# Block fetches behind the transposition, and u loaded in halves a step later

## The chip, the cores and the metric

One core of a Trainium2 chip. The time is the device time of one execution in microseconds (us). TensorE (PE) multiplies 128x128 weights with up to 512 columns into PSUM, VectorE (DVE) and ScalarE (ACT) do the elementwise work, SyncE (SP) and GpSimd (POOL) issue the DMAs. Each engine runs its own instructions in the order of the program and waits on semaphores for the others. SP's DMAs all go into one queue, worked off by 16 DMA engines.

## The reference

```python
def _attn_ref(u, v, z):                      # u, v: 4 x 3008 x 256, z: 4 x 3008 x 64
    scores = (1.0 / S) * np.matmul(z, z.transpose(0, 2, 1))
    attn = np.maximum(scores, 0.0) ** 2
    out = np.matmul(attn, v)
    return (u * out).astype(np.float32)

def _moe_ref(x, w_in, w_out):                # 12032 x 256, 256 x 2048, 2048 x 256
    h = x @ w_in
    relu6 = np.clip(h + 3.0, 0.0, 6.0)
    g = h * relu6 / 6.0
    return (g @ w_out).astype(np.float32)
```

The result is `_moe_ref(_attn_ref(u, v, z).reshape(12032, 256), w_in, w_out)`. All is done to float32 accuracy: each operand of a matmul is split into a rounded high and a low part.

## The kernel before, in words

**Work and order.** The order of all instructions is written out by hand in one loop over 288 steps (called g, from 0): 4 batches (b) of 6 chunks of 512 query tokens (c; the sixth has 448) of 12 pairs of 128-token key blocks (p). Step g multiplies the attention of pair g with v into two PSUM banks, `o0` and `o1` (d = 0 and 1, the halves of the 256 features), and computes the scores of pair g + 2. At the last step of a chunk, `times_u` (L560) multiplies `o0` and `o1` in place into the tile of u; only then may the first matmul of the next chunk write that bank.

**Mirrored blocks.** The score matrix is symmetric. A computed block that will be wanted transposed is stored to DRAM (`keep`, tiles `d`), later fetched with four DMAs (`fetch_pair`, L342, tile `l`, two buffers) and transposed on DVE (`turn`, L381, tile `rm`). Step g transposes the block of pair g + 3, ahead of which at most two fetched blocks wait; `fetch_mirrored` at the end of a step issues the next fetch where a buffer is free. In the sixth chunk ten of the twelve pairs are mirrored, ten steps in a row.

**MLP.** From step 33 on, every three steps hold one group: 128 x 2 of the 2048 hidden features of 1024 tokens (two chunks). A group's first step (on = 0) begins with two loads on SP, `wi` of the next group and `wo` of this one (L238, 896 and 512 KB). Its products `m` are spread over the three steps; its four `y` products (`down`) follow from the end of its third step. After 8 groups the output is scaled on ACT (L669) and stored (L672).

**u.** The tile of u has one buffer, for 1024 tokens: 1 MB, or 960 KB for a sixth chunk. After the last product with u, `split_x` turns the tile into the operands of the MLP in the first three steps behind a pair of chunks (`since` 1 to 3; the last subtraction, `xl` at L88, at the end of the third); then `load_u` (L552) fetches the next u. That load stands at the end of the third of these steps, three steps ahead of the step with the first products with the new u, which is the last one of the pair's first chunk. (The first two loads stand in steps 7 and 32.) The step after the load is always a group's first step (on = 0); in it SP also issues two stores of the computed blocks of the chunk's last pair (256 and 128 KB) and the output store of 512 KB.

**The code of a step** with on = 0: scores of pair g + 2 (first half), products with v for d = 0, `background()` (which transposes), the group's first part with the loads of `wi` and `wo`, the other half of the scores with the stores, products with v for d = 1, further parts of the group, `down()`, `fetch_mirrored()`, `load_u`. With on = 2 (the last step of a chunk): a part of the group, products for d = 0 and the first product with u, a part of the group, `down()`, scores, `background()`, scores, a part of the group, products for d = 1 and the second product with u, `down()`.

Of the kernel before, what the change touches and what calls it, by code (L numbers as in the profile page):

```python
# [7 lines left out]
F32 = mybir.dt.float32  # L8
# [7 lines left out]
P = 128  # L16
CH = 512
NCH = 6
# [9 lines left out]
SPLIT_FROM = 24  # L28
# [11 lines left out]
def relu2_attention_then_hswish_mlp(  # L40
# [24 lines left out]
    upool = ctx.enter_context(tc.tile_pool(name="upool", bufs=1))  # L65
# [234 lines left out]
    def flush():  # L300
        while late:
            late.pop(0)()
# [20 lines left out]
    to_fetch = []  # L323

    def fetch_mirrored():

        while to_fetch and len(mirrored) < 2:
            b, c, p = to_fetch[0]
            if (b, p // 2, c) not in whole:
                return  # L330
            fetch_pair(*to_fetch.pop(0))

    def fetch_pair(b, c, p):


        src = kept[b, p // 2, c]
        half = is_half(b, c, p)
        nk = 8 if half else width(c) // 32
        t = lpool.tile([P, 16, 64], F32, tag="l", name="l")
        for q in range(4):  # L340
            c0 = q * 64 if half else q * P + (p % 2) * 64
            nc.sync.dma_start(  # L342
                out=t[32 * q:32 * q + 32, :nk, :],
                in_=src[:, c0:c0 + 64].rearrange("(k e) f -> e k f", e=32),
            )
        mirrored[b, c, p] = t
# [195 lines left out]
    raw_x = {}  # L542

    def tokens(i):

        b, c = divmod(i, NCH // 2)
        return b * S + 2 * c * CH, width(2 * c) + width(2 * c + 1)

    def load_u(i):
        t0, n = tokens(i)  # L550
        t = raw_x[i] = upool.tile([P, 2, 2 * CH], F32, tag="u", name="u")
        nc.sync.dma_start(  # L552
            out=t[:, :, :n], in_=ut[:, t0:t0 + n].rearrange("(k p) t -> p k t", p=P)
        )

    def times_u(b, c, d):
# [7 lines left out]
    def split_x(i):  # L564


        raw = raw_x[i]
        n = tokens(i)[1] // 2
        left, right = raw[:, :, :n], raw[:, :, n:2 * n]
        new = xt[i] = {}  # L570

        def piece(k, src):
            shape = [P, 2, CH] if k < 3 else [P, CH]
            homes = ((xpool, f"xh{k}"), (xpool, f"xl{k}"))
            if i == NPR - 1:
                homes = ((apool, "ah"), (apool, "al")) if k < 3 else ((zpool, "zx"), (zpool, "zy"))
            xh, xl = (
                pool.tile(shape, F32R, tag=tag, name=f"x{w}{k}")
                for (pool, tag), w in zip(homes, "hl")
            )  # L580
            hi, lo = (x[:, :, :n] if k < 3 else x[:, :n] for x in (xh, xl))
            nc.scalar.copy(out=hi, in_=src)
            for r in range(2 if k < 3 else 1):
                new[2 * k + r] = (hi[:, r], lo[:, r]) if k < 3 else (hi, lo)
            return lambda: sub(lo, src, f(hi))

        if i < NPR - 1:
            pool, tag = (rpool, "r") if i else (hpool, "hb")
            t = pool.tile([P, 2, CH], F32, tag=tag, name="t")[:, :, :n]
        else:  # L590
            t = lpool.tile([P, 16, 64], F32, tag="l", name="t")
            t = t.rearrange("p k f -> p (k f)").rearrange("p (r n) -> p r n", r=2)[:, :, :n]
        sub(t[:, 0], right[:, 1], right[:, 0])
        sub(right[:, 0], right[:, 0], left[:, 0])
        sub(t[:, 1], right[:, 1], right[:, 0])
        yield
        low = piece(0, left)
        yield
        low()
        sub(left[:, 1], left[:, 1], t[:, 1])  # L600
        yield
        low = piece(2, t)
        yield
        low()
        yield
        low = piece(1, right)
        yield
        low()
        yield
        low = piece(3, left[:, 1])  # L610
        yield
        low()
        raw_x.pop(i)
        yield
# [207 lines left out]
    def turn_next():  # L822

        while g_turned[0] < min(g_done + 1, len(pairs)):
            turn(*pairs[g_turned[0]])
            g_turned[0] += 1

    def run(it, n=99):
        for _ in range(n):
            next(it, None)  # L830
# [9 lines left out]
    with tc.manual_schedule():  # L840
# [12 lines left out]
        second = scores(0, 0, 1, banks=("y10", "y11"))  # L853
# [5 lines left out]
        for i, (b, c) in enumerate(chunks):  # L859
            ahead = b + 1 if c == NCH - 1 and b + 1 < B else None  # L860
            for p in range(NPAIR):
                g = i * NPAIR + p
# [28 lines left out]

                def background():
                    turn_next()
                    if i == 0 and p == 7:
                        load_u(0)

                def prepare():
                    if ahead and p < NPAIR - 1:
# [18 lines left out]
                if on < 2 or at_mlp < 0:  # L917
# [5 lines left out]
                    else:  # L923
# [3 lines left out]
                        split_z(0, 2)  # L927
                    spare()
                    background()
                    run(unit, 1)  # L930
                    spare()
# [15 lines left out]
                else:  # L947
# [5 lines left out]
                    down()  # L953
                    run(nxt, 1)
                    background()
                    run(nxt, 1)
                    spare()
# [13 lines left out]
                done, since = divmod(g + 1 - AFTER, NFP * EVERY)  # L971
                if g == SPLIT_FROM:
                    xs = split_x(0)
                if SPLIT_FROM <= g < SPLIT_FROM + 9:
                    run(xs, 1)
                if g == SPLIT_FROM + 8:
                    load_u(1)
                if done > 1 and since in range(1, 4):
                    if since == 1:
                        xs = split_x(done - 1)  # L980
                    run(xs, 3)
                    if since == 3:
                        load_u(done)
        flush()
        xs = split_x(NPR - 1)
        left = range((len(pairs) - MLP_FROM) // EVERY, NPR * NFP)
# [96 lines left out]
```

## Time and profile before

| | |
|---|---|
| median of 3 runs | 1833.07 us (1832.08 to 1834.41) |
| the profiled execution | 1833.69 us, span 1831.9 us |
| granted TensorE clock, mean | 0.998 |
| PE busy | 1801.4 us (98%) |
| PEld (weight loads) | 1584.7 us (87%) |
| DVE | 1505.2 us (82%) |
| ACT | 1196.3 us (65%) |
| POOL | 55.2 us (3%) |
| DMA | mean 180 GB/s; SP's queue 60.8% of 16 engines' span |

Busy shares are of the span. A matmul's row shows some 0.38 us, since its ends are modelled and matmuls overlap; one of 512 columns starts every 0.215 us. In the rows, L73 is the helper of all matmuls and L88 that of all subtractions, so tiles tell them apart.

### The profile page before, as it was taken

To read this page: it belongs to the slowest core of one execution; us is meant where nothing else is said; L and a number is where in the kernel's file an instruction comes from. 1 tells how busy PE (TensorE), PEld (TensorE's weight loads), DVE (VectorE), ACT (ScalarE), POOL (GpSimd) and SP (SyncE) were. 2 spreads that over 40 slices of the span, in tenths; PEclk is the share of its full clock that TensorE was granted. 3 is DMA by queue.
4 is the path that set the end of the run, shared out by engine and by line. 5 is a ranking of instruction groups with operands and counts; after the bars stand their busy time and mean duration, and the time that the engine had idled before them with its cause. 6 is when DMAs were issued, how large, how long until landed. Compare 5 with 4: busy or idle time off the path is not lost.

```text
span 1831.9 us, 23310 instructions
## 1 busy us (share of the span) xinstructions
PE 1801.4 (98%) x8426; PEld 1584.7 (87%) x8426; DVE 1505.2 (82%) x1767; ACT 1196.3 (65%) x1640; POOL 55.2 (3%) x90
## 2 busy tenths in 40 slices
PE   8999999999999999999999999999999999999999
PEld 7877888988998888888899888888889988888888
DVE  8999988988778788897877877888877787787776
ACT  7896655767656555676766655667675665564565
POOL 1000000100000000010000000001000000000000
PEclk9999999999999999999999999999999999999999
DMA  8868896665664767856665667594565667676343
GB/s 227 242 220 264 212 221 183 188 190 172 183 159 140 193 168 152 229 161 202 186 178 135 177 176 178 130 258 151 160 202 144 173 186 175 143 171 162 109 167 128
DMA packets 440307, 329.50 MB, mean 180 GB/s; under 512 B 278656, under 2 KB 397440, under 8 KB 440192
## 3 DMA queue, kind: packets, MB, share of 16 engines
q1 hardware_dynamic: 432672, 304.16, 60.8%
q0 software_dynamic: 7520, 23.86, 4.5%
q8 instruction: 66, 1.08, 0.3%
q14 instruction: 49, 0.40, 0.1%
HBM read 241.70 MB, written 86.25 MB: 179 GB/s over the span
## 4 chain that ended last, share of the span: by engine, by line
PE 56%; issue 24%; DVE 11%; ACT 4%; DMA 2%; SPq 1%; POOL 0%; DVEq 0%; ACTq 0%; POOLq 0%
PE o L73 22%; PE y L73 16%; PE m L73 14%; PE s L73 5%; DVE al L88 2%; DMA l<-d 1%; DVE rm L381 1%; DVE gl L88 1%; DVE rb L706 1%; ACT gh L766 1%; DVE ra L706 1%; SPq L342 1%; DVE r L462 1%; DVE hb L91 1%; DVE xl L88 0%
## 5 line engine op out<-in xcount | busy, mean ns | idle before, releaser
L73 PE MATMUL m<-xh,wi 128*128 128x512 f32 (+1 forms) x1344 | 476.9, 378 | 8.0 <-DVE hb L91 4.4
L73 PE MATMUL o<-ah,vl 128*128 128x512 f32 (+1 forms) x1152 | 433.2, 376 | 9.8 <-DVE u L560 6.3
L73 PE MATMUL o<-ah,vh 128*128 128x512 f32 (+1 forms) x1152 | 432.0, 375 | 0.0
L73 PE MATMUL y<-gh,wo 128*128 128x512 f32 (+1 forms) x1536 | 388.6, 375 | 0.5 <-ACT gh L766 0.5
L73 PE MATMUL o<-al,vh 128*128 128x512 f32 (+1 forms) x1104 | 328.8, 376 | 2.9 <-DVE al L88 2.9
L73 PEld LDWEIGHTS y<-gh,wo 128*128 128x128 f32 x1536 | 289.9, 189 | 35.8 <-ACT gh L766 1.8
L73 PEld LDWEIGHTS m<-xh,wi 128*128 128x128 f32 x1344 | 254.9, 190 | 48.3 <-DVE hb L91 9.2
L73 PEld LDWEIGHTS o<-ah,vl 128*128 128x128 f32 x1152 | 217.7, 189 | 41.6 <-DVE u L560 8.7
L73 PE MATMUL m<-xl,wi 128*128 128x512 f32 (+1 forms) x672 | 252.4, 376 | 0.0
L73 PEld LDWEIGHTS o<-ah,vh 128*128 128x128 f32 x1152 | 218.0, 189 | 26.6
L73 PEld LDWEIGHTS o<-al,vh 128*128 128x128 f32 x1104 | 208.6, 190 | 30.0 <-DVE al L88 5.4
L73 PE MATMUL y<-gl,wo 128*128 128x512 f32 (+1 forms) x768 | 226.4, 376 | 0.9 <-DVE gl L88 0.5
L441 ACT ACTIVATE rt<-s 128x512 f32<-128x512 f32 (+1 forms) x310 | 180.0, 593 | 71.2 <-PE s L73 64.3
L462 DVE TENSOR_TENSOR r<-rt 128x1024 f32<-128x1024 f32 (+2 forms) x128 | 147.4, 1151 | 81.0 <-ACT rt L441 80.9
L747 ACT ACTIVATE ra<-m,three 128x512 f32<-128x512 f32 (+1 forms) x96 | 65.1, 678 | 174.9 <-PE m L73 132.0
L91 DVE TENSOR_TENSOR hb<-hb,m 128x512 f32<-128x512 f32 (+1 forms) x192 | 128.6, 670 | 59.7 <-PE m L73 59.0
L88 DVE TENSOR_TENSOR al<-r,ah 128x1024 fp32r<-128x1024 f32 (+3 forms) x147 | 164.3, 1118 | 5.7 <-ACT r L460 3.8
L469 ACT ACTIVATE ah<-rt 128x1024 fp32r<-128x1024 f32 (+1 forms) x155 | 163.7, 1056 | 4.9
L73 PEld LDWEIGHTS y<-gl,wo 128*128 128x128 f32 x768 | 144.7, 189 | 20.5 <-DVE gl L88 3.6
L88 DVE TENSOR_TENSOR gl<-rb,gh 128x1024 fp32r<-128x1024 f32 (+2 forms) x97 | 115.2, 1189 | 57.2 <-ACT gh L95 56.7
L381 DVE STREAM_TRANSPOSE rm<-l 128x1024 f32<-128x1024 f32 (+2 forms) x132 | 149.4, 1132 | 8.4 <-DMA l<-d 8.4
L88 DVE TENSOR_TENSOR al<-rm,ah 128x1024 fp32r<-128x1024 f32 (+1 forms) x132 | 155.2, 1176 | 1.3 <-ACT ah L408 0.9
(86 smaller groups left out, 2170.4 us busy)
## 6 DMA issues: line engine op xcount, KB each, us to landing
wi<-dwin SPq DMA_DIRECT2D x96, 896.0 KB, 5.4
d<-r SPq DMA_DIRECT2D x212, 256.0 KB, 3.2
wo<-dwout SPq DMA_DIRECT2D x96, 512.0 KB, 6.1
l<-d SPq DMA_DIRECT2D x304, 128.0 KB, 4.0
l<-d SPq DMA_DIRECT2D x160, 112.0 KB, 4.7
vraw<-in_v_dram POOLq DMA_DIRECT2D x33, 256.0 KB, 4.6
u<-in_ut_dram SPq DMA_DIRECT2D x8, 1024.0 KB, 5.4
out_dram<-y SPq DMA_DIRECT2D x16, 512.0 KB, 5.3
```

What stands on the lines that cost most here:

```text
L73: nc.tensor.matmul(out, lhsT=lhsT, rhs=rhs, start=start, stop=stop, skip_group_check=part)
L88: nc.vector.tensor_tensor(out=out, in0=a, in1=b, op=ALU.subtract)
L91: nc.vector.tensor_tensor(out=out, in0=a, in1=b, op=ALU.add)
L342: nc.sync.dma_start(out=t[32 * q:32 * q + 32, :nk, :], in_=src[:, c0:c0 + 64].rearrange("(k e) f -> e k f", e=32),)
L381: nc.vector.transpose(out=rn[:, :, :n].rearrange("p r (k e) -> p r k e", e=32), in_=t[:, :n // 32].rearrange("p k (r e) -> p r k e", r=2),)
L441: nc.scalar.activation(out=halved(rn[:, r]), in_=unpaired(s[:, :n]), func=AF.Relu, scale=1.0 / S)
L462: nc.vector.tensor_tensor(out=to, in0=of, in1=of, op=ALU.mult)
L469: nc.scalar.activation(out=hn, in_=rn, func=AF.Square)
L706: nc.vector.scalar_tensor_tensor(out=out, in0=out, scalar=6.0, in1=h, op0=ALU.min, op1=ALU.mult)
L747: nc.scalar.activation(out=ra[:, 1], in_=c21, func=AF.Relu, bias=three)
L766: nc.scalar.copy(out=ga[0], in_=ra)
```

## The change

`background()`, right behind the transposition, also calls `fetch_mirrored()` when the next block to fetch is one of a sixth chunk. `load_u` loads 512 columns at a time. For the third and later pairs of chunks the first half is issued at the end of the step behind the one where the whole load was, the second half seven steps after that. The first pair's second half comes twelve steps after its first, the second pair's eight steps.

```diff
-    def load_u(i):
+    def load_u(i, second):
+
         t0, n = tokens(i)
-        t = raw_x[i] = upool.tile([P, 2, 2 * CH], F32, tag="u", name="u")
+        if not second:
+            raw_x[i] = upool.tile([P, 2, 2 * CH], F32, tag="u", name="u")
+        cols = slice(CH, n) if second else slice(0, CH)
         nc.sync.dma_start(
-            out=t[:, :, :n], in_=ut[:, t0:t0 + n].rearrange("(k p) t -> p k t", p=P)
+            out=raw_x[i][:, :, cols],
+            in_=ut[:, t0 + cols.start:t0 + cols.stop].rearrange("(k p) t -> p k t", p=P),
         )
...
                 def background():
                     turn_next()
-                    if i == 0 and p == 7:
-                        load_u(0)
+                    if to_fetch and to_fetch[0][1] == NCH - 1:
+                        fetch_mirrored()
+                    if i < 2 and p == 7:
+                        load_u(0, i == 1)
...
-                if g == SPLIT_FROM + 8:
-                    load_u(1)
+                if g in (SPLIT_FROM + 8, SPLIT_FROM + 16):
+                    load_u(1, g == SPLIT_FROM + 16)
                 if done > 1 and since in range(1, 4):
                     if since == 1:
                         xs = split_x(done - 1)
                     run(xs, 3)
-                    if since == 3:
-                        load_u(done)
+                if done > 1 and since in (4, 11):
+                    load_u(done, since == 11)
```

## Rows read from the trace of the kernel before

**Rows 1.** Waits of PE: engine, tile and line, waited for: us in total, times, longest.
```profile
PE o L73 <- DVE u L560: 6.3, 4, 2.2
```
**Rows 2.** Timeline of PE around the four stops: start us, us, [idle before <-releaser].
```profile
300.48 1.03 PE L73 MATMUL y<-gh,wo 128*128 128x512 f32 x4
301.34 0.59 PE L73 MATMUL y<-gl,wo 128*128 128x512 f32 x2
...
305.96 0.52 PE L73 MATMUL o<-ah,vl 128*128 128x448 f32 x1 [2.24 <-DVE u L560]
...
754.78 0.46 PE L73 MATMUL o<-ah,vl 128*128 128x448 f32 x1 [0.86 <-DVE u L560]
...
1202.34 0.46 PE L73 MATMUL o<-ah,vl 128*128 128x448 f32 x1 [1.19 <-DVE u L560]
...
1650.63 0.46 PE L73 MATMUL o<-ah,vl 128*128 128x448 f32 x1 [2.04 <-DVE u L560]
```
**Rows 3.** Timeline of DVE ahead of the four stops, the first batch's in detail.
```profile
288.62 1.10 DVE L381 STREAM_TRANSPOSE rm<-l 128x896 f32<-128x896 f32 x1
...
298.50 0.68 DVE L560 TENSOR_TENSOR u<-u,o 128x512 f32<-128x512 f32 x1
...
303.09 1.11 DVE L381 STREAM_TRANSPOSE rm<-l 128x896 f32<-128x896 f32 x1 [2.77 <-DMA l<-d]
...
305.23 0.68 DVE L560 TENSOR_TENSOR u<-u,o 128x512 f32<-128x512 f32 x1
...
751.91 1.11 DVE L381 STREAM_TRANSPOSE rm<-l 128x896 f32<-128x896 f32 x1 [1.39 <-DMA l<-d]
...
1199.47 1.11 DVE L381 STREAM_TRANSPOSE rm<-l 128x896 f32<-128x896 f32 x1 [1.71 <-DMA l<-d]
...
1647.76 1.11 DVE L381 STREAM_TRANSPOSE rm<-l 128x896 f32<-128x896 f32 x1 [2.57 <-DMA l<-d]
```
**Rows 4.** Waits of SP's own queue, the load of u (L552) alone.
```profile
SPq L552 <- DVE xl L88: 80.2, 10, 8.8
```
**Rows 5.** Timeline of SP, 287 to 294 us: issues of u, wi, wo, output.
```profile
287.59 0.40 SPq L552 DMA_DIRECT2D u<-in_ut_dram  x1
288.08 0.41 SPq L238 DMA_DIRECT2D wi<-dwin  x1
288.59 1.84 SPq L238 DMA_DIRECT2D wo<-dwout  x1
...
293.18 0.40 SPq L672 DMA_DIRECT2D out_dram<-y  x1
```
**Rows 6.** Stretches: from:to, us, busy of each engine, PEclk, DMA share, GB/s.
```profile
289.50:303.01 13.51, 13.51 (x65) 11.98 (x64) 9.64 (x13) 8.13 (x12) 0.00 (x0) 1.00 1.06 305
306.30:309.60 3.30, 3.30 (x10) 2.85 (x9) 2.77 (x3) 1.41 (x3) 0.00 (x0) 0.50 0.99 245
309.70:1651.00 1341.30, 1333.27 (x6293) 1182.27 (x6293) 1093.96 (x1219) 862.79 (x1172) 36.28 (x57) 1.00 0.65 175
```
**Rows 7.** DMA view, 287.5 to 293.3 (last row: 276.8 to 278.8): KB each, us to landing.
```profile
GB/s 0 0 0 0 0 0 0 132 298 132 106 132 53 106 159 291 318 371 371 318 371 371 424 424 424 424 397 447 420 440 574 198 521 471 323 422 323 445 346 494
...
u<-in_ut_dram SPq DMA_DIRECT2D x1, 960.0 KB, 5.7
wi<-dwin SPq DMA_DIRECT2D x1, 896.0 KB, 8.5
wo<-dwout SPq DMA_DIRECT2D x1, 512.0 KB, 9.2
out_dram<-y SPq DMA_DIRECT2D x1, 512.0 KB, 7.2
...
l<-d SPq DMA_DIRECT2D x4, 112.0 KB, 2.8
```
**Rows 8.** SP and DVE in the narrowest of the six other places.
```profile
891.99 0.56 SPq L672 DMA_DIRECT2D out_dram<-y  x1
...
898.89 0.68 DVE L560 TENSOR_TENSOR u<-u,o 128x512 f32<-128x512 f32 x1
```

## The prediction

> **What bounds the kernel now.** I read the busy shares first: TensorE (PE) is busy 98% of a span of 1831.9 us, so a gain can only come out of its few stops. The list of PE's waits comes next: the largest entry is an `o` matmul waiting for the in-place product with u, 6.3 us in four stops [rows 1]. The PE timeline places them: 305.96, 754.78, 1202.34 and 1650.63 us, that is 2.24, 0.86, 1.19 and 2.04 us, always at the first step of a sixth chunk [rows 2]. The VectorE (DVE) timeline says why [rows 3]: in the step before, the transposition of a fetched block stands idle until its fetch lands (2.77, 1.39, 1.71, 2.57 us), and the second u product, which frees the bank PE wants, is queued behind it. The SyncE (SP) rows say why the fetch is late. SP stood 8.8 us in front of the u load, waiting for the last subtraction of the activation split [rows 4]; then u, wi, wo, two stores and an output store were issued within 6 us, and the block fetch only behind them, at 293.6 [rows 5]. From there to the landing of the blocks the DMA engines were saturated: 305 GB/s, share 1.06 [rows 6]. The clock rows finish the picture: behind the 2.24 us stop the granted clock is 0.50 for 3.41 us, the lower level of 1.2 GHz; so it is behind the 2.04 us one, and between these two stretches it is 1.00, the stops of 0.86 and 1.19 us included [rows 6]. At half clock 3.41 us cost 1.71 us of work.
>
> So all that this change can win is 6.3 + 2 x 1.71 = 9.7 us. Nowhere else did a transposition wait for its fetch.
>
> **The change part by part.** I call T the end of the transposition in the step two steps before the sixth chunk (289.72 = 288.62 + 1.10 in the first batch [rows 3]); the same order repeats in the four batches within 0.1 us up to the wait.
>
> *The moved fetch.* In the steps whose next block belongs to a sixth chunk, the four DMAs of a fetch are issued behind the transposition instead of at the end of the step. DVE's and PE's orders don't change; SP's does: wi, wo, stores and output of that step now stand behind DMAs that wait for T. At the place of the stop this brings the fetch from 293.6 to 289.7. Four such DMAs, issued over 1.9 us with 2.8 us to landing in a quiet queue [rows 7], land at T + 1.4 + 2.8 = T + 4.2 = 293.9, 6.4 us before DVE asks for them. The l wait is gone for good: minus 8.4 us of DVE waits. The other nine fetches of each sixth chunk had not been late, so nothing is won there. The price: wi and wo are issued at T + 1.9 and T + 2.4 instead of 1.6 and 1.1 us before T [rows 5]. At this place wo would land about T + 9 (behind wi, as below), and its first use is the `y` matmul at 300.48, T + 10.8 [rows 2]: hidden, with under 2 us to spare. Bounds: 0 and, with the 9.2 us of [rows 7], T + 11.6, 0.8 us late. I take 0.
>
> *u a step later.* SP no longer stands in front of u for the split: 80.2 us of SP waiting in ten places [rows 4], which by itself costs PE nothing. But the first half is now the last thing that step issues: behind the fetch, wi, wo, both stores and the output store (which waits for ScalarE until 293.18 [rows 5]). And its reader has not moved: the first u product stood at 298.50, T + 8.78 [rows 3]. Until now u was first in that queue and landed at 287.59 + 5.7 = 293.3, 5.2 us early. So when does half a u land as the last of it? The blocks at T + 4.2. Then wi, wo, the two stores and the output: before, the same five ran from the landing of u at 293.3 to 293.18 + 7.2 = 300.4: 7.1 us [rows 5, 7]; the three other batches give 6.4 to 6.6, and I take 6.7. Then 512 KB of u: wo's 512 KB landed 297.8 - 296.6 = 1.2 us behind wi, and the 896 KB of stores and output took 300.4 - 297.8 = 2.6 us, 1.5 for each 512 KB [rows 5, 7]; I take 1.4. Sum: T + 12.3, bounds T + 11.8 (6.4 + 1.2) and T + 12.8 (7.1 + 1.5). **u is late by 12.3 - 8.78 = 3.5 us** in each of the four places. A DVE wait on u takes the place of the one on l, and it is longer: 4 x 3.5 = 14.0 against 8.4.
>
> *The six other late loads* (first and third pair of chunks) have no fetch in that step; wi and wo are issued early and have landed. There u goes out some 0.5 us behind the output store, and lands about 5 us after that store's issue (2.8 to landing for small DMAs in a quiet queue, plus 1.5 and some 0.7 for the two 512 KB). The tightest of the six: store at 891.99, product at 898.89 [rows 8], so 2 us to spare. Cost 0; if that cover were gone, each would cost what it is late.
>
> *The second halves* go out seven steps before their use, the first two loads twelve and more steps or as before: 1.4 us of queue, nobody near. Cost 0.
>
> *What PE sees.* With R the time at which DVE would take up the delayed transposition without a wait (303.09 - 2.77 = 300.32, T + 10.6): before, PE's stopped matmul started at R + wait + 2.87 (305.96). After, the wait of 3.5 lies ahead of the first u product. Behind it stands the product that gives `gl`, which ends R + 3.5, and PE needs `gl` for the `y` matmuls at 301.34, R + 1.02 [rows 2, 3]. So PE stops earlier and longer, 2.5 us, above both stops that were followed by half clock. I take a half-clock stretch at all four places: PE has 2.38 us of work from there to the `o` matmul (301.34 to 305.96 - 2.24); 0.26 us of it run before the drop, 1.71 us in the 3.41 us at half, 0.42 behind: the `o` matmul starts at R + 3.5 + 0.26 + 3.41 + 0.42 = R + 7.6. Before, with the 1.71 us lost behind the two longer stops, it counts as R + 2.77 + 2.87 + 1.71 = 7.35, R + 4.26, R + 4.58 and R + 7.15. Differences: 0.3 + 3.3 + 3.0 + 0.5 = **7.1 us longer**. By the bounds of u's landing: 4 x 0.5 either way, 5 to 9; with no more half-clock stretches than before 5.6 - 1.4 = about 4.
>
> Against the profiled execution (1833.69 us, 0.6 above the median of the runs) that is 1840.8; against the median of 1833.07, 1840.2. I write 1840.
>
> **A rule weighed.** Over those 13.5 us the queue ran at 305 GB/s [rows 6]; the 2816 KB from wi to half of u (896 + 512 + 256 + 128 + 512 + 512) take 8.1 us in my sum, 356 GB/s, since the slow 256-byte rows of the blocks are out of it. The Trainium skill ("DMA: Bandwidth & Descriptors", Where 436 GB/s comes from) puts the ceiling of the SBUF ports at 435 GB/s and says that some 358 bind for traffic from HBM. An estimate by these figures: T + 12.3 for u at 358, as my sum, and T + 10.8 at 435. That single slices do come near 435, and past it, speaks against my sum, and is the first rival.
>
> **The rivals.**
>
> 1. *The queue runs faster*: at the 424 GB/s of its fast slices [rows 7] those 2816 KB take 6.8 us, and u lands at T + 11.0, late by 2.2. PE stops for 1.2 us, no half clock anywhere, the `o` matmul at R + 2.2 + 2.87 = R + 5.07. Against 7.35, 4.26, 4.58 and 7.15: -2.3 + 0.8 + 0.5 - 2.1 = -3.1 us, 1830. For it: no 960 KB load runs ahead. Against: the five took 6.4 us or more in all four batches, and half of u comes on top. Chance 0.14.
> 2. *u is in time*: the halves land by T + 8.8, all four stops and both half-clock stretches go: 9.7 us less, 1823.4. It needs u to overtake what is issued ahead of it, or those loads to go out before T. Against: every landing in [rows 7] follows the order of issue (u 293.3, wi 296.6, wo 297.8, the output 300.4). Chance 0.12.
> 3. *Slower still: wo becomes the late one.* In three group steps of each batch wo now stands behind a fetch that waits for DVE. It decides where wo needs more than 8.4 us from its issue at T + 2.4 to its use at T + 10.8. At 9.2 [rows 7] it is 0.8 us late; at eight places besides the four that u hides, 6 us on top: 1846, and with the upper bounds 1849. Chance 0.10.
> 4. *The change doesn't do what it says*: the fetch finds no free buffer and stays at the step's end. Then wi and wo, freed of the wait for the split, land before T, and u comes behind the stores, the output (293.2 + 2.8 + 1.5) and 448 KB of blocks at some 1.3 us, plus 1.4: 300.2, late by 1.7, no half clock: 4 x (1.7 + 2.87) = 18.3 against 23.3, 1828. But the transposition takes its block off the list that is counted just ahead of the call, so the buffer is free: a hundredth, counted with rival 2.
>
> **How the numbers follow.** The forecast has 0.64. Some 0.2%, 3.7 us, is what a measurement of this kernel tells from no change. Slower by more: 0.56 of the forecast's cases (the rest stay under 3.7 with fewer half-clock stretches) and rival 3: 0.66. Within: 0.08 and half of rival 1: 0.15. Faster: the rest of rival 1, rival 2: 0.19. The range reaches from 1825, which holds rival 1 and leaves most of rival 2 out, to 1849; the forecast's own is 1836 to 1844.
>
> **What would show it.** Right: in the DVE timeline, one step ahead of each sixth chunk, a wait of some 3.5 us in front of the first u product, ended by the DMA of u, and none in front of the transposition; on PE a stop at the `y` matmuls with `gl`, and four half-clock stretches instead of two; on SP no wait for the split at the u loads. Wrong: PE's four stops gone and the clock at 1.00 throughout (rival 2), or short stops without a clock drop (rival 1). A wait at `y` for wo, more than one per batch, is rival 3. My forecast fails if the five transfers ahead of u take less than 5.5 us.

## The result: slower by 1.0%, and the profile after

The changed kernel takes 1851.61 us (median of 4 runs, 1848.83 to 1853.8) against 1832.57 us beside it: a ratio of 1.0100, 95% interval 1.0087 to 1.0113. That is 19.0 us more, where 7 were forecast; the time lies above the range. The profiled execution took 1852.05 us, its span is 1850.3 us.

The waits of PE after (who, waited for: us in total, times, longest) have no `o` matmul behind a u product any more, the entry of [rows 1]. Two others lead instead:

```profile
PE y L73 <- DVE gl L88: 17.2, 5, 5.8
PE y L73 <- DMA wo<-dwout: 5.8, 4, 3.8
```

The stops on PE's timeline, which answer to [rows 2], stand at the `y` matmuls. Four are at the end of the step ahead of a sixth chunk; the ones at 340.50 and 794.40 us come six steps later, inside the chunk:

```profile
304.77 0.48 PE L73 MATMUL y<-gl,wo 128*128 128x512 f32 x1 [3.39 <-DVE gl L88]
...
340.50 0.45 PE L73 MATMUL y<-gh,wo 128*128 128x512 f32 x1 [1.59 <-DMA wo<-dwout]
...
756.72 0.80 PE L73 MATMUL y<-gl,wo 128*128 128x512 f32 x1 [3.34 <-DVE gl L88]
...
794.40 0.76 PE L73 MATMUL y<-gh,wo 128*128 128x512 f32 x1 [3.79 <-DMA wo<-dwout]
...
1212.84 0.48 PE L73 MATMUL y<-gl,wo 128*128 128x512 f32 x1 [4.14 <-DVE gl L88]
...
1666.46 0.79 PE L73 MATMUL y<-gl,wo 128*128 128x512 f32 x1 [5.82 <-DVE gl L88]
```

DVE's timeline, the counterpart of [rows 3], shows what is late. The first u product waits for the DMA of u in all four batches; the delayed transposition of before (now at 304.64) starts without a wait:

```profile
288.50 1.10 DVE L381 STREAM_TRANSPOSE rm<-l 128x896 f32<-128x896 f32 x1
...
302.90 0.69 DVE L564 TENSOR_TENSOR u<-u,o 128x512 f32<-128x512 f32 x1 [4.43 <-DMA u<-in_ut_dram]
303.50 1.22 DVE L88 TENSOR_TENSOR gl<-ra,gh 128x1024 fp32r<-128x1024 f32 x1
304.64 1.10 DVE L381 STREAM_TRANSPOSE rm<-l 128x896 f32<-128x896 f32 x1
...
754.84 0.69 DVE L564 TENSOR_TENSOR u<-u,o 128x512 f32<-128x512 f32 x1 [4.38 <-DMA u<-in_ut_dram]
...
1210.96 0.69 DVE L564 TENSOR_TENSOR u<-u,o 128x512 f32<-128x512 f32 x1 [5.18 <-DMA u<-in_ut_dram]
...
1664.59 0.69 DVE L564 TENSOR_TENSOR u<-u,o 128x512 f32<-128x512 f32 x1 [7.27 <-DMA u<-in_ut_dram]
```

One transposition still waits for its fetch, 1.9 us at 798.48, inside the second batch's sixth chunk.

SP's timeline of the step with the late u, which answers to [rows 5], has u as the last of the group, behind the fetch that waits for the transposition:

```profile
289.63 1.87 SPq L342 DMA_DIRECT2D l<-d  x4
291.60 0.42 SPq L238 DMA_DIRECT2D wi<-dwin  x1
292.12 0.38 SPq L238 DMA_DIRECT2D wo<-dwout  x1
...
294.25 0.57 SPq L676 DMA_DIRECT2D out_dram<-y  x1
294.87 0.62 SPq L555 DMA_DIRECT2D u<-in_ut_dram  x1
```

The DMA view of that stretch (KB each, us from issue to landing) puts u's landing at 294.87 + 7.9 = 302.8, 1.6 us behind the output store's 294.25 + 6.9 = 301.15:

```profile
out_dram<-y SPq DMA_DIRECT2D x1, 512.0 KB, 6.9
u<-in_ut_dram SPq DMA_DIRECT2D x1, 512.0 KB, 7.9
```

Where [rows 6] had one of two half-clock stretches, there are now five, one of them 6.8 us long (from:to, us, busy of each engine, PEclk, DMA share, GB/s):

```profile
305.70:309.10 3.40, 3.40 (x10) 2.91 (x9) 3.40 (x5) 1.41 (x2) 0.00 (x0) 0.50 0.61 137
756.30:759.60 3.30, 2.88 (x7) 2.52 (x8) 3.30 (x5) 0.78 (x1) 0.00 (x0) 0.50 0.48 145
793.90:797.20 3.30, 2.80 (x7) 2.29 (x8) 2.68 (x3) 1.04 (x1) 0.71 (x1) 0.50 1.09 236
1213.70:1217.00 3.30, 3.30 (x11) 2.81 (x10) 3.30 (x5) 1.12 (x2) 0.00 (x0) 0.50 0.58 132
1664.30:1671.00 6.70, 4.54 (x12) 3.82 (x12) 6.41 (x7) 1.05 (x1) 0.00 (x0) 0.50 0.45 120
```

PE's order is the same in both kernels, so the start of the same matmul can be compared. The changed kernel falls behind by 1.2, 3.9, 4.6 and 4.7 us at the four u waits (14.4 us), and by 1.7, 4.7 and 0.3 us at the stops for wo (6.8 us before rounding); 2.6 us come back in small pieces elsewhere. The span is 18.6 us longer by the last matmul.

### The profile page after: what moved, and what is told of

Read it like the earlier page. It is cut to its first block, busy times and chain, and to the rows that moved or that the text cites. A ratio compares the mean times of both kernels' runs of the same rounds, so it can differ in the third digit from the quotient of the medians.

```text
span 1850.3 us, 23327 instructions
## 1 busy us (share of the span) xinstructions
PE 1804.7 (98%) x8426; PEld 1588.9 (86%) x8426; DVE 1506.3 (81%) x1767; ACT 1196.2 (65%) x1640; POOL 55.3 (3%) x90
## 4 chain that ended last, share of the span: by engine, by line
PE 78%; DVE 9%; DMA 6%; issue 3%; ACT 2%; SPq 1%; DVEq 0%; ACTq 0%
PE o L73 31%; PE y L73 22%; PE m L73 19%; PE s L73 6%; DMA l<-d 2%; DMA wo<-dwout 2%; DVE al L88 2%; DMA vraw<-in_v_dram 1%; DVE rm L381 1%; DVE gl L88 1%; DVE hb L91 1%; SPq L342 1%; DVE rb L710 1%; DVE r L462 1%; DMA u<-in_ut_dram 1%
```

## The experiments

Theory Q: u is late because it is the last of what one step puts into SP's queue, and wo because it stands behind a fetch that waits for DVE. Rival S: the moved fetch itself costs, u is its victim. Rival H: the halves themselves are slow. Rival L: a step later is too late, wherever the load stands. Ratios are against the kernel before, with 95% intervals.

| kernel | median us | ratio | DVE waits for u, us |
|---|---|---|---|
| the change | 1851.61 | 1.0100 (1.0087 to 1.0113) | 21.3 |
| e1 fetch moved, u as before | 1831.12 | 0.9992 (0.9978 to 1.0006) | 0 |
| e2 u as in the change, fetch as before | 1834.16 | 0.9999 (0.9985 to 1.0012) | 12.5 |
| e3 change, first half at the old place | 1829.09 | 0.9982 (0.9970 to 0.9994) | 0 |
| e4 change, fetch behind wi and wo | 1830.38 | 0.9982 (0.9971 to 0.9992) | 9.1 |
| e5 change, fetch moved in one step only | 1847.81 | 1.0083 (1.0068 to 1.0098) | 19.1 |
| e6 change, u ahead of wi | 1825.93 | 0.9969 (0.9955 to 0.9982) | 0 |
| e7 change, u whole | 1855.38 | 1.0119 (1.0102 to 1.0136) | 25.2 |
| e8 e5 and e3 together | 1826.60 | 0.9967 (0.9954 to 0.9980) | 0 |
| e9 change, u behind wi and wo | 1830.86 | 0.9992 (0.9979 to 1.0006) | 7.8 |
| e10 e5 and e6 together | 1825.47 | 0.9962 (0.9949 to 0.9975) | 0 |

**e1, the fetch alone.** The moved fetch of the change with u loaded whole at its old place (the call for a second half returns at once; the DMA line, left out here, is the old one):

```diff
-        if not second:
-            raw_x[i] = upool.tile([P, 2, 2 * CH], F32, tag="u", name="u")
-        cols = slice(CH, n) if second else slice(0, CH)
+        if second:
+            return
+        t = raw_x[i] = upool.tile([P, 2, 2 * CH], F32, tag="u", name="u")
...
-                if done > 1 and since in (4, 11):
+                if done > 1 and since in (3, 11):
```

> The fetch is moved as in the change, u is loaded whole and at its old place. Theory Q (u is late because it is the last of six transfers in SP's queue, wo because it stands behind a fetch that waits for DVE): u is first in the queue again and lands before its product, the fetch lands in time, so all four stops in front of the sixth chunk go, -9.7 us; the wo stops ten groups of matmuls later stay, +5 to +7 us. Sum 1828 to 1831. Rival S (the moved fetch is what costs, by holding up SP, and u is only its victim): slower than before by most of the 19 us, 1845 to 1852.

Measured 1831.12, the upper edge of Q's numbers; S is out. The u stops are gone. PE waits at `y` for wo, 3.6 us in two stops, and the 2.40 us one is followed by half clock. A third stop of 1.76 us (336.49) belongs to them: the list puts it down to ScalarE, but it ends 0.14 us behind wo's landing (327.64 + 8.71 = 336.35), as the other two do. Together they are 5.3 us, the 5 to 7 that Q had; why they come from the fetch is taken up below.

**e2, u alone.** The fetch in `background()` taken out:

```diff
                     turn_next()
-                    if to_fetch and to_fetch[0][1] == NCH - 1:
-                        fetch_mirrored()
```

> u in halves and a step later as in the change, the fetch at the end of its step as before. Theory Q: wi and wo no longer stand behind a wait, land before the stores, and nothing is late for wo; the first half of u comes behind stores, output and fetch, lands some 1.5 us late, stops of 0.5 to 1 us without half clock: 1826 to 1829. Rival S: 1823 to 1824, since without the moved fetch nothing is late. Rival H (the halves themselves are slow, or a step later is too late by itself): u late by 3 us or more, 1840 and above.

Measured 1834.16, between Q's numbers and H's. Its trace shows where my sum was short: the first half of u stands behind stores, output and fetch and takes 4.2, 4.5, 6.2 and 6.4 us from issue to landing in the four batches, so DVE waits 2.0, 2.3, 4.0 and 4.2 us for it, not 1.5. (The profiled execution, 1838.25 us, is the slowest of the ten.) Neither half of the change costs 19 us by itself: each alone is level with the kernel before.

**e3, the half not a step later.**

```diff
-                if done > 1 and since in (4, 11):
+                if done > 1 and since in (3, 11):
```

> Fetch moved, u in halves, the first half at its old place instead of a step later. Theory Q: the half is first in the queue and in time, as in the kernel with the fetch alone: no u stop, wo stops of 5 to 7 us stay: 1828 to 1831. Rival H (halves are slow by themselves): u stops remain, 1840 and above. Rival S: 1845 and above.

As Q: 1829.09, no wait for u. Halves are not what costs (H). The waits for wo came out smaller than expected, 1.0 us in its profile; that execution, 1826.39 us, is the fastest of the ten, so the others may have more.

**e4, the weights first.** The moved fetch called behind the group's first part, so behind wi and wo (in a step with on = 2, right behind `background()`):

```diff
                 def background():
                     turn_next()
+                    if i < 2 and p == 7:
+                        load_u(0, i == 1)
+
+                def fetch_early():
                     if to_fetch and to_fetch[0][1] == NCH - 1:
                         fetch_mirrored()
-                    if i < 2 and p == 7:
-                        load_u(0, i == 1)
...
                     background()
                     run(unit, 1)
+                    fetch_early()
```

> All of the change, but the moved fetch is issued behind the group's first part, so behind wi and wo, and still ahead of stores, output and u. Theory Q: wi and wo land before the transposition ends, u has only the fetch, two stores and the output ahead of it and lands about 8 us behind the transposition, in time by under 1 us; wo is never late: 1822 to 1827. Rival S: the fetch is as early as before in all but three steps of ten, so most of the loss stays, 1840 and above. Rival H: u late all the same, 1838 and above.

S is out again, at 1830.38, and wo is in time everywhere. I had expected u in time too, and it is not: the first u product waits 1.9 to 3.0 us in all four batches (its list puts two of these waits down to a PE matmul that had ended long before; they end 0.1 us behind u's landing). In the first batch u is issued at 293.44 and lands 7.0 us later, 2.8 us behind an output store that landed in 4.6; in the others it lands 3.1, 3.7 and 3.2 us behind that store:

```profile
out_dram<-y SPq DMA_DIRECT2D x1, 512.0 KB, 4.6
u<-in_ut_dram SPq DMA_DIRECT2D x1, 512.0 KB, 7.0
```

**e5, the fetch moved in one step.**

```diff
-                    if to_fetch and to_fetch[0][1] == NCH - 1:
+                    if to_fetch and to_fetch[0][1] == NCH - 1 and c == NCH - 2 and p == NPAIR - 3:
```

> The change with the fetch moved only in the step that ends up with u late (two steps ahead of the sixth chunk); the other nine fetches of each sixth chunk at the end of their steps as before. Theory Q splits the loss of the change into two parts: u last behind the fetch, wi, wo, stores and output at one step of each batch (about 14 us), and wo behind the fetch at the later group steps (about 5 us). Here the first part stays and the second goes: 1844 to 1848, with the stops at the y matmuls waiting for wo gone. Rival (all of it is u): 1850 to 1853.

1847.81: the u waits stay (19.1 us), wo is in time everywhere. By the medians that part is worth 3.8 us, though the two intervals overlap. Stops of 2.1 and 0.7 us at the same `y` matmuls remain, for another reason: in the first of these steps ScalarE and, behind it, DVE waited for a load of v, and the cast that feeds the matmul came late (ScalarE's waits for v, then PE's timeline):

```profile
ACT vh L95 <- DMA vraw<-in_v_dram: 5.7, 5, 2.9
```
```profile
342.23 0.48 PE L73 MATMUL y<-gh,wo 128*128 128x512 f32 x1 [2.13 <-ACT gh L770]
```

In e8, which moves the same one fetch and has u in time, these stops are gone. So a late u shifts the whole crowd of transfers of that later step as well.

**e6, u ahead of the weights.** Still a step later, but inside `background()`, behind the moved fetch:

```diff
                     if to_fetch and to_fetch[0][1] == NCH - 1:
                         fetch_mirrored()
+                    if since_now == 4 and done_now > 1:
+                        load_u(done_now, False)
```

> All of the change, with the first half of u still a step later, but issued right behind the moved fetch, so ahead of wi, wo, stores and output. Theory Q (place in the queue): u lands some 6 us behind the transposition, 2 us and more ahead of its product, so no stop at u; wo half a us to 1 us later than in the change: 1828 to 1833. Rival L (a step later is too late, wherever it stands): u stops stay, 1845 and above.

1825.93, better than expected: 25.7 us below the change, by the place of one DMA per pair of chunks. SP's timeline, and the landing of u 4.5 us after its issue at 291.45, 296.0:

```profile
289.49 1.87 SPq L342 DMA_DIRECT2D l<-d  x4
291.45 0.42 SPq L555 DMA_DIRECT2D u<-in_ut_dram  x1
291.98 0.41 SPq L238 DMA_DIRECT2D wi<-dwin  x1
292.48 0.38 SPq L238 DMA_DIRECT2D wo<-dwout  x1
```
```profile
u<-in_ut_dram SPq DMA_DIRECT2D x1, 512.0 KB, 4.5
```

L is out: the step later is harmless at this place. The stops for wo have not gone, 3.5 us in five, the longest 1.84 us (782.14; its list puts it down to ScalarE, but it ends 0.14 us behind wo's landing), and no half clock follows them.

**e7, twice the bytes at the end of the queue.** The change with u whole at `since == 4`.

> All of the change, but u whole at the place of its first half, so twice the bytes (960 KB or 1 MB) at the end of the same queue. Theory Q: u lands 1.3 to 2.5 us later than in the change at each of the four places, each at full price: 1856 to 1862; the other six places keep up to 1 us of margin. Rival H (halves themselves cost): no slower than the change, 1852 or less.

1855.38, just under Q's numbers and above H's 1852; the interval of its ratio overlaps that of the change, so against H e3 is the stronger evidence. Its waits for u are 6.2, 6.6, 6.4 and 6.0 us, 6.3 in the mean against 5.3 in the change. The 448 KB more at the end of the queue count with 1 us in the mean and with 1.7 us in the first three batches; the fourth batch's wait, the longest of the change, is shorter here.

**e9, a middle place.** The load behind wi and wo, ahead of the stores and the output:

```diff
                     run(unit, 1)
+                    if since_now == 4 and done_now > 1:
+                        load_u(done_now, False)
```

> All of the change, with the first half of u issued in the same step right behind wi and wo, ahead of the two stores and the output store: a middle place in the queue. Theory Q (each transfer ahead of u costs its own queue time): u lands some 2.5 to 3 us earlier than in the change, so the waits of VectorE on u shrink from 4.3 to 7.3 us to 1.8 to 3.5 us, stops of 1 to 2.5 us with half clock at some; the wo stops stay: 1835 to 1842, between the change and the kernel with u ahead of wi. Rival (only what waits for ScalarE or the fetch matters, the length of the queue doesn't): either no stop at u, 1826 to 1830, or as the change, 1850 and above.

The waits for u, 2.7, 1.6, 1.8 and 1.8 us, are what Q said or shorter; the time, 1830.86, is below Q's numbers. One reason is in the clock row of its profiled span, where Q had expected half clock at some stops: 1.00 throughout.

```profile
5.10:1827.00 1821.90, 1793.13 (x8419) 1579.36 (x8417) 1503.46 (x1763) 1194.07 (x1637) 51.17 (x79) 1.00 0.65 180
```

Its DMA view lists the landings of wi, wo and u in the order of issue: wo at 291.73 + 7.7 = 299.4, u at 292.20 + 8.5 = 300.7, so half a u costs 1.3 us behind wo.

```profile
wi<-dwin SPq DMA_DIRECT2D x1, 896.0 KB, 6.7
wo<-dwout SPq DMA_DIRECT2D x1, 512.0 KB, 7.7
u<-in_ut_dram SPq DMA_DIRECT2D x1, 512.0 KB, 8.5
```

**e8 and e10, the better versions.** e8 is e5 with the first half at `since == 3`; e10 is e5 with the load of e6.

> A version meant to beat both: the fetch moved only in the one step two ahead of the sixth chunk, u in halves with the first half at its old place and the second seven steps behind the split. Theory Q: neither l, u nor wo is late: the four stops of before and both half-clock stretches go, 1823 to 1826, some 3 us below the kernel with all ten fetches moved and the half not later. If a measured gain stays under 4 us, something besides those stops sets the time there.

> A version meant to beat all: the first half of u right behind the moved fetch and ahead of wi, a step later than before, and the fetch moved in that one step only. Theory Q: the stops of before, those at wo and the short ones at the products of the sixth chunk are all gone: 1822 to 1825, 2 to 4 us below the kernel with the half at its old place, no half clock.

1826.60 and 1825.47: 0.3 to 0.4% below the kernel before, clear of it. Both are just above their expected numbers. e8 has none of the four stops and no half clock:

```profile
7.70:1823.00 1815.30, 1792.36 (x8413) 1578.33 (x8411) 1502.91 (x1761) 1193.54 (x1636) 50.19 (x77) 1.00 0.66 181
```

e8, e10 and e6 lie within each other's intervals. In its profiled execution e10 kept one stop of 2.4 us inside a sixth chunk with half clock behind it; the mean clock of its other four runs is 1.000, so half clock does not explain its median.

## Why the prediction was right in direction and wrong in size

*The moved fetch, the place of u in the queue, the new wait, the stop at `gl`: right.* The blocks land 6 us early, SP no longer waits for the split, DVE waits at the first u product and not at the transposition, PE stops at the `y` matmuls and the clock falls at all four places. The first three of these stops, 3.39, 3.34 and 4.14 us, are within 0.02 us the waits less the 1.02 us of the prediction's sum; the fourth, 5.82 us, is 0.4 us shorter than that. e6 and e3 show it from the other side: change only u's place, and all of the loss goes.

*The landing of u, "T + 12.3, bounds T + 11.8 and T + 12.8": too early, and above the upper bound in all four batches.* It landed at 302.8, T + 13.2, in the first batch; the waits of 4.4, 4.4, 5.2 and 7.3 us stand at T + 13.2, 13.2, 14.0 and 16.1 (T + 8.8 and the wait). Two terms of the sum were too small. The five transfers ahead took 7.2, 7.3, 6.7 and 9.1 us where I took 6.7, and half of u landed 1.6, 1.6, 2.5 and 2.6 us behind the output store where I took 1.4; the blocks came up to 0.5 us later than T + 4.2. That size of u's last term I had from wo behind wi; behind an output store it is 1.6 to 2.6 here and 2.8 to 3.7 in e4. What made the fourth batch the worst stays open. Its wi landed 5.3 us behind the blocks, against 2.6 to 3.4 in the others, but in that time the queue moved 329 GB/s, or 1.75 MB, nearly twice wi itself, so it did not stand still (from:to, us, busy of each engine, PEclk, DMA share, GB/s):

```profile
1652.81:1658.14 5.33, 5.33 (x27) 4.66 (x26) 3.37 (x5) 2.46 (x4) 0.00 (x0) 1.00 1.02 329
```

The price of a late u that the prediction worked out held: 21.3 us of waits instead of 14.0 add 7.3 to the 7.1 us, 14.4, and 14.4 were measured. By place its sum gives 1.2, 4.2, 4.7 and 4.2 us with the measured waits, against 1.2, 3.9, 4.6 and 4.7, so that the totals agree so closely is partly luck.

*"I take 0" for wo: wrong at the later group steps.* At the place of the stop it was right: wo landed at 292.12 + 6.6 = 298.7 and was in time. I priced the other two group steps of the sixth chunk by the same distance, T + 10.8, without reading theirs. At the first of the places where it stopped, the trace of the kernel before has T + 9.5, from 328.24 to 337.77 (DVE's timeline, then PE's):

```profile
327.14 1.10 DVE L381 STREAM_TRANSPOSE rm<-l 128x896 f32<-128x896 f32 x1
```
```profile
337.77 0.48 PE L73 MATMUL y<-gh,wo 128*128 128x512 f32 x1
```

After the change that transposition ends at 329.3 and wo lands at 332.03 + 8.3 = 340.3, T + 11.1, 1.6 us late (DMA view, with GpSimd's v in the same crowd); in the second batch wo takes 10.75 us there and is 3.8 us late:

```profile
wi<-dwin SPq DMA_DIRECT2D x1, 896.0 KB, 5.9
wo<-dwout SPq DMA_DIRECT2D x1, 512.0 KB, 8.3
vraw<-in_v_dram POOLq DMA_DIRECT2D x1, 256.0 KB, 8.0
```

That the fetch ahead of wi and wo makes wo late shows across the runs. In the six kernels where all ten moved fetches stand ahead of them (the change, e1, e3, e6, e7, e9) `y` matmuls stop for 1.0 to 5.8 us in all until wo has landed, whether u is late or not. In the five others (e2, e4, e5, e8, e10) it is 0.2 us or nothing.

That was rival 3, of chance 0.10 and 6 us: it came on top of the forecast, 6.8 us, and not in its stead, and nearly all of it at two places, not at eight. The two terms, 7.3 and 6.8 us, less the 2.6 us that come back, are the 11.5 us between the 7.1 us forecast and the 18.6 of the two profiles.

*The rule weighed.* By 358 GB/s (the Trainium skill, "DMA: Bandwidth & Descriptors", Where 436 GB/s comes from) the 2816 KB from wi to u would have taken 8.1 us, an estimate. In the first batch they ran from about T + 4.4 to T + 13.2, 8.8 us, 330 GB/s; in the fourth they took 11.7 us. The measurement decides: for these loads and stores in one queue the Trainium skill's figure was a bound that was not reached. Rival 1, a faster queue, and rival 2, u in time, did not occur.

## What to carry to other kernels

A DMA moved to a later place in a queue is priced by all that now stands ahead of it, counted from the moment the first of those can start, and by the distance to its reader, which has not moved. Taking a wait off the head of a queue is worth nothing if the load then leaves last: here one DMA's place was worth 25.7 us, and the same edit with u five DMAs earlier gains where it lost. Every instruction that a moved DMA passes needs its own reader's distance read from the trace, not the first one's.

## What the runs showed that I had not expected

The price of a stop is not its length. With DVE waiting 7.8 us in all for u (e9) there was no half clock in its profile and the kernel was level with before; at 21.3 us there were five half-clock stretches and it was 19 us slower. Between the two the waits for u grew by 13.5 us and the time by 20.8. Stops of PE up to 1.84 us were not followed by half clock in any of these profiles. Of those between 1.9 and 2.4 us most were, one of 1.91 us in e4 among them, but one of 2.26 us in e9 was not (PE's timelines of e4 and e9):

```profile
1198.85 0.48 PE L73 MATMUL y<-gl,wo 128*128 128x512 f32 x1 [1.91 <-DVE gl L88]
```
```profile
337.88 0.45 PE L73 MATMUL y<-gh,wo 128*128 128x512 f32 x1 [2.26 <-DMA wo<-dwout]
```

The longest stop of the change, 5.82 us, was followed by two such stretches in a row, 6.8 us; but in e5 a stop of 3.37 us was too, and one of 4.24 us by a single one. That may be why runs of one kernel differ: e6's ten spread over 9.5 us with mean clocks from 0.998 to 1.000, while e8's five, whose profile has no stop above 0.5 us at a `y` matmul, spread over 0.8 us, all at 1.000. Only one trace of each is kept, so this is not shown.
